# Two decode attentions side by side: part of one weight load and the two output stores move from SP's DMA queue to GpSimd's

## The chip, the cores and the metric

The kernel runs on one core of a Trainium2 chip. The time is device microseconds of one execution; the time of a version is the median of several runs. The runs before took 249.95, 250.19 and 251.74 us, median 250.19. One more execution was taken by the hardware profiler; it took 250.0 us, and its trace gives all other times here.

## What is computed

Two independent attention blocks, A and B, each for one new token (batch 1, one query position) and a model width of 576: project to 32 query heads of 128, attend over 16 heads of a key and value cache (two query heads share one), and project back to 576. A sees the last 2048 positions of its cache, B all 8192. All tensors are bfloat16. The two results are put side by side.

```python
def _A_ref(x, k_cache, v_cache, wq, wo):
    W = min(4096, max(256, Sk // 4))                       # 2048
    q = (x @ wq).reshape(B, Sq, Hq, Dh) ...
    k = jnp.repeat(k_cache[:, :, Sk - W:, :], rep, axis=1)  # B: the whole cache
    v = jnp.repeat(v_cache[:, :, Sk - W:, :], rep, axis=1)
    p = _softmax(jnp.einsum("bhqd,bhkd->bhqk", q, k) * (Dh ** -0.5), axis=-1)
    o = jnp.einsum("bhqk,bhkd->bhqd", p, v)
    return o ... .reshape(B, Sq, Hq * Dh) @ wo
...
return jnp.concatenate([a, b], axis=-1)
```

## The kernel before

The kernel is written by hand, engine by engine. `Prog` (lines 32 to 104) holds one list of operations for each engine; `op` adds a compute instruction and `load` a DMA, each with the names it depends on. `emit` (54) writes the lists out in that order: an engine waits with `wait_ge` for the semaphores that its next instruction needs and has not yet seen. A DMA adds 16 to a semaphore of its own. So the order on each engine, and on the queue that issues its DMAs, is the order of the calls in the source.

**Loads.** All large loads go out from SP. `place` (167) hands out space in `ring`, an area of 144 KB in each of the 128 partitions, in turn; a load waits until the users of what lay there before are done. The order is: A's wq (line 198, the first 512 rows as 128 partitions of 32 KB, and line 200, the other 64 rows as 128 partitions of 4 KB), B's wq in the same two parts, then for each pair of heads p = 0 to 7 the K of B (208, 128 partitions of 32 KB), the K of A (211, twice 4 KB), the V of B, the V of A, and then wo of A (219, one load of 36 KB a partition) and wo of B in six loads, the last two of 1152 bytes a partition. The two x rows, 1152 bytes each, go out from ACT (189).

**GpSimd.** It issues no DMA. It makes the constants at the start (229 to 242): a row of ones, the identity `ident`, then `identf` (235), and the memsets of `zb` (236), `za` (237), `mexp`, `onesf` and `pts` (240), last the permutation `perm` (241).

**Projection.** x is replicated over columns by matmuls with a row of ones (272), after VectorE has doubled the tail of x into `xdup` (263), and copied to `xrep` (275, 278). Then come eight groups of matmuls for A and eight for B (`qmm`, line 295), five matmuls of 512 columns each; they wait for their weights by name (297). ACT and VectorE bring the sums out (301, 304), VectorE transposes them (306) and places them in `za` and `zb` (318, 312). The projections' end frees the ring space of wq, for which SP's load of A's first V (211) waits.

**Attention.** For each pair p VectorE transposes ten slabs of K in the ring (335), PE multiplies them with the queries (345); a maximum, an exponential (380), transposes of the weights (384), the product with V (393, 400) and a fold into `ob` (414, 421) follow.

**End.** After the sums are divided out, PE projects with wo (457), first A, then B in six steps as its loads land. For each of the two, ACT and VectorE copy one row each into `outsb` (465, 468), and SP stores the two rows of 576 bytes (469, `out0` and `out1`). SP's last step (473) waits for both stores.

The steps of the prediction touch the issue of A's wq (198), GpSimd's list (229 to 241), the wait of `qmm` (297) and the stores (469).

Of the kernel before, what the change touches and what calls it, by code (L numbers as in the profile page):

```python
# [31 lines left out]
class Prog:  # L32
# [9 lines left out]
    def op(self, eng, fn, deps=(), name=None):  # L42
        self.ops[eng].append((fn, tuple(deps), name, None))
        if name is not None:
            assert name not in self.where, name
            self.where[name] = (eng, len(self.ops[eng]) - 1)

    def load(self, eng, fn, sem, value, deps=(), name=None):
        self.ops[eng].append((fn, tuple(deps), None, sem))
        if name is not None:  # L50
            assert name not in self.dma, name
            self.dma[name] = (sem, value)
# [54 lines left out]
def bass_concat_heads__sliding_block_cached__gqa_block_cached__decode_kernel(nc, A_x, A_k_cache, A_v_cache, A_wq, A_wo,  # L107
# [51 lines left out]
    op, load = pg.op, pg.load  # L159
    s_x = [nc.alloc_semaphore("s_x%d" % i) for i in range(2)]  # L160
    s_ld = [nc.alloc_semaphore("s_ld%d" % i) for i in range(NSEM)]
    s_out = nc.alloc_semaphore("s_out")


# [2 lines left out]
    def place(size, uses, issue, name):  # L167
        if at[0] + size > RING:
            at[0] = 0
        lo, hi = at[0], at[0] + size  # L170
        at[0] = hi
        deps = []
        for r in list(live):
            if r[0] < hi and lo < r[1]:
                deps += r[2]
                live.remove(r)
        n = nload[0]
        nload[0] += 1
        if n >= NSEM:
            deps += uses_of[n - NSEM]  # L180
        uses_of.append(list(uses))
        live.append((lo, hi, list(uses)))
        t = ring[:, lo:hi]
        load("sp", lambda e: issue(e, t), s_ld[n % NSEM], 16 * (n // NSEM + 1), deps=deps, name=name)
        return t
# [7 lines left out]
    wq_at = {}  # L193
    w = HQ * DH
    for P in range(2):
        uses = ["qmm%d.7" % P]
        main = wqs[P][0:512, :].rearrange("(p k) n -> p (k n)", k=4)
        wq_at[P, 0] = place(4 * w, uses, lambda e, t, main=main: e.dma_start(t, main), "wq%d.0" % P)
        tail = wqs[P][512:DM, :].rearrange("r (c n) -> (r c) n", c=2)
        wq_at[P, 1] = place(w // 2, uses, lambda e, t, tail=tail: e.dma_start(t, tail), "wq%d.1" % P)  # L200

    kv_at = {}
    for p in range(NP):
        for kind, c in (("K", ks), ("V", vs)):
# [3 lines left out]
                                      lambda e, t, src=src: e.dma_start(t, src), "%sB%d" % (kind, p))  # L208
            src = c[0][0, 2 * p:2 * p + 2, SK - W_A:SK, :].rearrange("h (q t) d -> q h (t d)", q=128)
            kv_at[kind, p, 1] = place(2 * SLAB, [use % (p, NI - 1)],  # L210
                                      lambda e, t, src=src: e.dma_start(t.rearrange("q (h n) -> q h n", h=2), src),
# [11 lines left out]
    def slab(kind, p, s):  # L223
# [9 lines left out]
       deps=["id0"], name="ident")  # L233
# [12 lines left out]
    for c in range(2):  # L246
        op("dve", lambda e, c=c: e.tensor_reduce(par[:, c:c + 1], view(identf, 128, c, [[2, 64]]), AX.X, ALU.add),
           deps=["identf"], name="par%d" % c)
    for h in range(2):
        op("dve", lambda e, h=h: e.tensor_reduce(  # L250
            cls[:, 2 * h:2 * h + 2], view(identf, 128, 64 * h, [[1, 2], [32, 2], [2, NB]]), AX.XY, ALU.add),
            deps=["identf"], name="clsB%d" % h)
    op("dve", lambda e: e.tensor_reduce(cls[:, 4:8], view(identf, 128, 2 * NB, [[1, 4], [32, 4]]), AX.X, ALU.add),
       deps=["identf"], name="clsA")
    op("dve", lambda e: e.tensor_reduce(selb[:], view(identf, 128, 0, [[1, 16], [32, 4]]), AX.X, ALU.add),
       deps=["identf"], name="selb")
    op("dve", lambda e: e.tensor_reduce(sela[:], view(identf, 128, 0, [[4, 2], [1, 2], [32, 4], [2, 2]]), AX.XY, ALU.add),
       deps=["identf"], name="sela")
# [3 lines left out]
    for P in range(2):  # L262
# [14 lines left out]
        for c in range(2):  # L277
            op("dve", lambda e, P=P, c=c: e.tensor_scalar(  # L278
                xrep[:, P, 4 + c, :], banks[2 * P + 1][:, 0:128], par[:, c:c + 1], None, ALU.mult),
                deps=["xT%d.4" % P, "par%d" % c], name="xr%d.%d" % (P, 1 + c))  # L280
    XR = ["xr%d.%d" % (P, c) for P in range(2) for c in range(3)]

    KT = NKT * SLAB
    for P in range(2):
        for n in range(8):
            u = 8 * P + n
            bank = banks[u % 4]

            def mm(e, P=P, n=n, bank=bank):
                for k in range(5):  # L290
                    if k < 4:
                        lhsT, o = xrep[:, P, k, :], wq_at[P, 0][:, k * w + n * 512:k * w + (n + 1) * 512]
                    else:
                        lhsT, o = xrep[:, P, 4 + n // 4, :], wq_at[P, 1][:, (n % 4) * 512:(n % 4 + 1) * 512]
                    ins = e.matmul(bank[:, :], lhsT=lhsT, rhs=o, start=(k == 0), stop=(k == 4))  # L295
                return ins
            op("pe", mm, deps=["wq%d.0" % P, "wq%d.1" % P] + XR + (["qe%d" % (u - 4)] if u >= 4 else []),
               name="qmm%d.%d" % (P, n))
            deps = ["qmm%d.%d" % (P, n)] + (["qT%d" % (u - 2)] if u >= 2 else [])
            if n % 2 == 0:  # L300
                op("act", lambda e, n=n, bank=bank: e.activation(qsb[:, n % 2, :], bank[:, :], ACT.Copy),  # L301
                   deps=deps, name="qe%d" % u)
            else:
                op("dve", lambda e, n=n, bank=bank: e.tensor_copy(qsb[:, n % 2, :], bank[:, :]),
                   deps=deps, name="qe%d" % u)
            op("dve", lambda e, n=n: e.transpose(  # L306
                ktb[:, n * 512:(n + 1) * 512].bitcast(I32), qsb[:, n % 2, :].bitcast(I32)),
                deps=["qe%d" % u] + (["z0.%d" % i for i in range(8)] if P else []), name="qT%d" % u)
        srcs = [[512, NP], [64, 2], [1, 2], [128, 2]]
        for b in range(4):  # L310
            if P == 1:
                op("dve", lambda e, b=b: e.tensor_copy(
                    view(zb, NP * 4 * ZW, 32 * b + W0, [[4 * ZW, NP], [2 * ZW, 2], [ZW, 2], [1, 2]], 32, 32 * b),
                    view(ktb, KT, b // 2 * 256, srcs, 32, 32 * b)),
                    deps=["qT%d" % u for u in range(8, 16)] + ["zb0"], name="z1.%d" % b)
            else:
                for h in range(2):
                    op("dve", lambda e, b=b, h=h: e.tensor_copy(
                        view(za, NP * 1024, h * 512 + 32 * b + 2 * (NB + h),
                             [[1024, NP], [256, 2], [128, 2], [1, 2]], 32, 32 * b),  # L320
                        view(ktb, KT, h * 256, srcs, 32, 32 * b)),
                        deps=["qT%d" % u for u in range(8)] + ["za0"], name="z0.%d" % (2 * b + h))
# [6 lines left out]
    for p in range(NP):  # L329
        for s in range(NI):  # L330
            k = p * NI + s
            kt = ktb[:, (k % NKT) * SLAB:(k % NKT + 1) * SLAB]
            deps = [unit("K", p, s)]
            deps += ["S%d" % (k - NKT)] if k >= NKT else Z
            op("dve", lambda e, p=p, s=s, kt=kt: e.transpose(kt.bitcast(I32), slab("K", p, s).bitcast(I32)),  # L335
               deps=deps, name="T%d.%d" % (p, s))
# [12 lines left out]
            deps = ["T%d.%d" % (p, s)]  # L349
# [5 lines left out]
           deps=["S%d" % (p * NI + NI - 1)] + (["mT%d" % (p - 1)] if p else []), name="max%d" % p)  # L355
        op("pe", lambda e: e.matmul(mb[0:1, 0:128], lhsT=mx[:, 0:1], rhs=identf[:, :], start=True, stop=True),  # L356
           deps=["max%d" % p, "identf"] + (["mrA%d" % (p - 1), "mrB1.%d" % (p - 1), "nb%d" % (p - 1)] if p else []),
           name="mT%d" % p)
        deps = ["mT%d" % p] + (["bc%d" % (p - 1)] if p else ["mexp0"])
        for h in range(2):  # L360
            op("dve", lambda e, h=h: e.tensor_reduce(
                mr[0:1, 2 * h:2 * h + 2], view(mb, 512, 64 * h, [[1, 2], [32, 2], [2, NB]], parts=1), AX.XY, ALU.max),
                deps=deps + (["mxB%d.%d" % (h, p - 1)] if p else []), name="mrB%d.%d" % (h, p))
        op("dve", lambda e: e.tensor_reduce(
            mr[0:1, 4:8], view(mb, 512, 2 * NB, [[1, 4], [32, 4]], parts=1), AX.X, ALU.max),
            deps=deps + (["mxA%d" % (p - 1)] if p else []), name="mrA%d" % p)
        for h in range(2):
# [3 lines left out]
                deps=["mrB%d.%d" % (h, p)], name="mxB%d.%d" % (h, p))  # L371
# [3 lines left out]
            deps=["mrA%d" % p], name="mxA%d" % p)  # L375
        op("pe", lambda e: e.matmul(mb[:, 128:129], lhsT=mexp[0:1, :], rhs=onesf[0:1, 0:1], start=True, stop=True),
           deps=["mxA%d" % p, "mxB0.%d" % p, "mxB1.%d" % p, "ones"], name="bc%d" % p)
        op("dve", lambda e, p=p: e.tensor_copy(nb[:, p % 2:p % 2 + 1], mb[:, 128:129]),  # L378
           deps=["bc%d" % p] + (["exp%d" % (p - 2)] if p >= 2 else []), name="nb%d" % p)
        op("act", lambda e, p=p: e.activation(psb[:, :], sb[p % 2][:, :], ACT.Exp, bias=nb[:, p % 2:p % 2 + 1],  # L380
                                              scale=SCALE, accum_out=rsall[:, p:p + 1]),
           deps=["nb%d" % p, "warm1"] + (["PT0.%d" % (p - 1), "PT1.%d" % (p - 1)] if p else []), name="exp%d" % p)
# [67 lines left out]
    for P in range(2):  # L450
        k0 = 0
        for c, kk in enumerate(NWO[P]):
            def mm(e, P=P, c=c, k0=k0, kk=kk):
                for k in range(kk):
                    for n in range(2):
                        r = 32 * (2 * P + n)
                        ins = e.matmul(fb[r:r + 1, 0:288], lhsT=oP[:, 1 - P, k0 + k:k0 + k + 1],  # L457
                                       rhs=wo_at[P, c][:, k * DM + 288 * n:k * DM + 288 * n + 288],
                                       start=(k0 + k == 0), stop=(k0 + k == HQ - 1))
                return ins  # L460
            op("pe", mm, deps=["wo%d.%d" % (P, c), "oP"] + ["qe%d" % u for u in range(16)], name="F%d.%d" % (P, c))
            k0 += kk
        done = "F%d.%d" % (P, len(NWO[P]) - 1)
        r = 64 * P
        op("act", lambda e, r=r: e.activation(outsb[r:r + 1, :], fb[r:r + 1, 0:288], ACT.Copy),
           deps=[done], name="f%d.0" % P)
        r = 64 * P + 32
        op("dve", lambda e, r=r: e.tensor_copy(outsb[r:r + 1, :], fb[r:r + 1, 0:288]), deps=[done], name="f%d.1" % P)
        load("sp", lambda e, P=P: e.dma_start(
            out[0, 0:1, P * DM:(P + 1) * DM].rearrange("o (n c) -> (o n) c", n=2),  # L470
            bass.AP(tensor=outsb, offset=64 * P * 288, ap=[[32 * 288, 2], [1, 288]])),
            s_out, 16 * (P + 1), deps=["f%d.0" % P, "f%d.1" % P], name="out%d" % P)
# [32 lines left out]
```

## Time and profile before

| what | value |
|---|---|
| median of three runs | 250.19 us |
| the profiled execution | 250.0 us |
| its span, from the first to the last instruction | 248.2 us |
| busy: PE, VectorE, ACT, GpSimd | 181.7, 153.1, 18.1, 13.4 us |
| mean DMA rate | 415 GB/s, 102.92 MB |
| mean granted TensorE clock | 0.82 |
| median from issue to landing, K and V of B | 27.0 and 26.8 us |

How to read the profile: times are microseconds from the start of the span. A page has rows of 40 digits, one for each fortieth of the span (6.2 us); a digit is the busy share in tenths, 9 being 90% or more. A row of the timeline has the start, the time, the engine (`PE` matmul, `PEld` weight load, `DVE` VectorE, `POOL` GpSimd, `SPq` the instruction of SP that issues a DMA), the line, the operation with output and input, and in brackets how long the engine had been idle and what released it. The chain of waits is followed back from the last instruction, at each step to what released it. A row of stretches has its bounds and length, the busy time and the number of instructions of PE, weight loads, VectorE, ACT and GpSimd, then the granted clock, the share of the DMA engines, and GB/s.

The chain by lines, as the page sums it up:

```profile
DMA ring<-in_B_k_cache_dram 22%; DVE ktb L335 18%; DMA ring<-in_B_wo_dram 10%; PE sb L345 10%; PE vb L393 7%; DVE xdup L263 5%; PE sb L295 4%; PE qb L295 3%; DVE pts L384 3%; ACT psb L380 2%; PE ob L414 1%; DVE mx L354 1%; PE ob L421 1%; PE vb L400 1%; PE mb L356 1%
```

### The profile page before, as it was taken

The numbers are of one execution on the slowest core, as the hardware profiler recorded it, in microseconds if no ns is written. First come the engines' busy times: TensorE is split into PE (matmuls) and PEld (weight loads), VectorE is DVE, ScalarE is ACT, GpSimd is POOL, SyncE is SP. The second block draws the span as 40 slices with busy tenths as digits, with TensorE's granted clock in tenths as the row PEclk, the third lists the DMA queues.
The fourth block names the chain that finished last, engine by engine and source line by source line (L and its number), as shares of the span: only waits on it lengthen the run. The fifth ranks groups of instructions, "written<-read, shape, count | busy, mean of one in ns | idle before, by whom it ended". The sixth has DMA issues, their size and how long they took to land.

```text
span 248.2 us, 2581 instructions
## 1 busy us (share of the span) xinstructions
PE 181.7 (73%) x1085; PEld 80.7 (33%) x1085; DVE 153.1 (62%) x228; ACT 18.1 (7%) x36; POOL 13.4 (5%) x15
## 2 busy tenths in 40 slices
PE   0039994957995799379746984998489757975795
PEld 0013441313631342143224321732153124322552
DVE  8963779952885298439734873487349725972300
ACT  2001220010001000100010001000100010001000
POOL 8920000000000000000000000000000000000000
PEclk9999999795589599877987597569677957895769
DMA  7999999999999999999999999999999999999992
GB/s 264 418 490 433 422 422 416 417 428 418 427 414 434 419 458 419 436 432 431 421 429 414 434 422 428 420 422 419 433 420 433 428 433 422 436 403 457 395 406 111
DMA packets 8262, 102.92 MB, mean 415 GB/s; under 512 B 694, under 2 KB 956, under 8 KB 5564
## 3 DMA queue, kind: packets, MB, share of 16 engines
q1 hardware_dynamic: 8248, 102.77, 97.9%
q8 instruction: 8, 0.13, 0.2%
q14 instruction: 2, 0.02, 0.0%
q10 hardware_dynamic: 4, 0.00, 0.0%
HBM read 102.76 MB, written 0.00 MB: 414 GB/s over the span
## 4 chain that ended last, share of the span: by engine, by line
DMA 32%; DVE 31%; PE 30%; issue 3%; ACT 2%; SPq 0%; POOL 0%; POOLq 0%; DVEq 0%
DMA ring<-in_B_k_cache_dram 22%; DVE ktb L335 18%; DMA ring<-in_B_wo_dram 10%; PE sb L345 10%; PE vb L393 7%; DVE xdup L263 5%; PE sb L295 4%; PE qb L295 3%; DVE pts L384 3%; ACT psb L380 2%; PE ob L414 1%; DVE mx L354 1%; PE ob L421 1%; PE vb L400 1%; PE mb L356 1%
## 5 line engine op out<-in xcount | busy, mean ns | idle before, releaser
L335 DVE STREAM_TRANSPOSE ktb<-ring 128x1024 int32<-128x1024 int32 x80 | 92.4, 1213 | 11.3 <-DMA ring<-in_B_k_cache_dram 7.6
L345 PE MATMUL sb<-ktb,zb 128*128 128x512 bf16 x256 | 73.6, 443 | 11.0 <-DVE ktb L335 9.8
L345 PEld LDWEIGHTS sb<-ktb,zb 128*128 128x128 bf16 x256 | 25.6, 110 | 56.3 <-DVE ktb L335 24.2
L393 PE MATMUL vb<-ring,pts 128*16 128x512 bf16 x256 | 28.2, 619 | 21.1 <-DVE pts L384 21.1
L409 DVE COPY xo<-vb 128x512 f32<-128x512 f32 x8 | 5.5, 692 | 35.8 <-PE vb L400 35.8
L393 PEld LDWEIGHTS vb<-ring,pts 128*16 128x16 bf16 x256 | 8.5, 123 | 34.3 <-issue 34.2
L345 PE MATMUL sb<-ktb,za 128*128 128x512 bf16 x64 | 16.7, 381 | 1.3
L380 ACT ACTIVATE psb<-sb,nb 128x512 bf16<-128x512 f32 x8 | 5.5, 687 | 140.9 <-DVE nb L378 140.9
L384 DVE STREAM_TRANSPOSE pts<-psb 64x512 bf16<-64x512 bf16 x16 | 11.3, 706 | 7.0 <-ACT psb L380 6.8
L295 PE MATMUL sb<-ring,xrep 128*128 128x512 bf16 x40 | 11.2, 438 | 1.3 <-DVE xrep L278 1.3
L263 DVE COPY xdup<-xrow 1x128 bf16<-1x128 bf16 x2 | 11.3, 5660 | 0.0
L457 PE MATMUL qb<-ring,oP 128*1 128x288 bf16 x128 | 10.9, 346 | 0.5 <-DVE oP L446 0.4
L414 PEld LDWEIGHTS ob<-selb,xo 128*128 128x128 f32 x64 | 10.1, 242 | 3.4 <-ACT xo L407 3.4
L354 DVE TENSOR_REDUCE mx<-sb 128x1 f32<-128x512 f32 x8 | 5.5, 692 | 9.1 <-PE sb L345 9.1
L414 PE MATMUL ob<-selb,xo 128*128 128x4 f32 x64 | 10.8, 293 | 0.3 <-ACT xo L407 0.3
L272 PE MATMUL sb<-onesb,xrow 1*128 1x128 bf16 x4 | 0.6, 295 | 14.0 <-DVE xdup L263 14.0
L306 DVE STREAM_TRANSPOSE ktb<-qsb 128x256 int32<-128x256 int32 x16 | 7.0, 443 | 6.1 <-ACT qsb L301 5.8
L421 PE MATMUL ob<-sela,xo 128*128 128x2 f32 x64 | 9.9, 276 | 0.0
L421 PEld LDWEIGHTS ob<-sela,xo 128*128 128x128 f32 x64 | 9.5, 227 | 0.0
L295 PE MATMUL qb<-ring,xrep 128*128 128x512 bf16 x40 | 9.3, 379 | 0.0
L345 PEld LDWEIGHTS sb<-ktb,za 128*128 128x128 bf16 x64 | 4.9, 96 | 13.1 <-DVE ktb L335 9.2
L457 PEld LDWEIGHTS qb<-ring,oP 128*1 128x1 bf16 x128 | 6.1, 99 | 5.3 <-DMA ring<-in_B_wo_dram 1.2
(66 smaller groups left out, 83.0 us busy)
## 6 DMA issues: line engine op xcount, KB each, us to landing
ring<-in_B_k_cache_dram SPq DMA_DIRECT2D x8, 4096.0 KB, 27.0
ring<-in_B_v_cache_dram SPq DMA_DIRECT2D x8, 4096.0 KB, 26.8
ring<-in_A_k_cache_dram SPq DMA_DIRECT2D x8, 1024.0 KB, 28.9
ring<-in_A_v_cache_dram SPq DMA_DIRECT2D x8, 1024.0 KB, 27.2
ring<-in_A_wo_dram SPq DMA_DIRECT2D x1, 4608.0 KB, 28.2
ring<-in_A_wq_dram SPq DMA_DIRECT2D x1, 4096.0 KB, 12.2
ring<-in_B_wq_dram SPq DMA_DIRECT2D x1, 4096.0 KB, 22.3
ring<-in_B_wo_dram SPq DMA_DIRECT2D x1, 2304.0 KB, 33.4
```

What stands on the lines that cost most here:

```text
L263: op("dve", lambda e, P=P: e.tensor_copy(view(xdup, 256, 128 * P, [[2, 64], [1, 2]], parts=1), view(xrow, 2 * DM, P * DM + 512, [[1, 64], ...
L295: ins = e.matmul(bank[:, :], lhsT=lhsT, rhs=o, start=(k == 0), stop=(k == 4))
L306: op("dve", lambda e, n=n: e.transpose(ktb[:, n * 512:(n + 1) * 512].bitcast(I32), qsb[:, n % 2, :].bitcast(I32)), deps=["qe%d" % u] + ([" ...
L335: op("dve", lambda e, p=p, s=s, kt=kt: e.transpose(kt.bitcast(I32), slab("K", p, s).bitcast(I32)), deps=deps, name="T%d.%d" % (p, s))
L345: ins = e.matmul(sb[p % 2][:, :], lhsT=lhsT, rhs=view(ktb, KT, (k % NKT) * SLAB + 64 * c + v, [[128, 16], [2, 32]]), start=(s == 0 and c = ...
L354: op("dve", lambda e, p=p: e.tensor_reduce(mx[:, 0:1], sb[p % 2][:, :], AX.X, ALU.max), deps=["S%d" % (p * NI + NI - 1)] + (["mT%d" % (p - ...
L380: op("act", lambda e, p=p: e.activation(psb[:, :], sb[p % 2][:, :], ACT.Exp, bias=nb[:, p % 2:p % 2 + 1], scale=SCALE, accum_out=rsall[:, ...
L384: op("dve", lambda e, h=h: e.transpose(view(pts, 1024, 2 * h, [[4, 16], [64, 16], [1, 2]], 64, 64 * h), psb[64 * h:64 * h + 64, :]), deps= ...
L393: ins = e.matmul(vb[0][32 * j:32 * j + 16, :], lhsT=view(pts, 1024, 64 * s + 16 * j, [[1, 16]]), rhs=src[:, 512 * j:512 * j + 512], start= ...
L414: ins = e.matmul(ob[:, 8 * p:8 * p + 4], lhsT=xo[:, 0, 128 * t:128 * t + 128], rhs=selb[:, 4 * t:4 * t + 4], start=(t == 0), stop=(t == 3))
L421: ins = e.matmul(ob[:, 8 * p + 4 + 2 * h:8 * p + 6 + 2 * h], lhsT=xo[:, 1, 256 * h + 128 * t:256 * h + 128 * t + 128], rhs=sela[:, 2 * t:2 ...
L457: ins = e.matmul(fb[r:r + 1, 0:288], lhsT=oP[:, 1 - P, k0 + k:k0 + k + 1], rhs=wo_at[P, c][:, k * DM + 288 * n:k * DM + 288 * n + 288], st ...
```

## The change

The 128 partitions of A's first wq load are divided. SP loads partitions 32 to 127 (3 MB), GpSimd partitions 0 to 31 (1 MB) with a semaphore of its own. GpSimd's load is the first entry of its list, ahead of the constants. All 16 projection groups name it among what they wait for. Both stores are issued by GpSimd, after its constants; SP's last step still waits for them. No other instruction is added, removed or put in another place, and the bytes moved are the same.

```diff
+    s_wq = nc.alloc_semaphore("s_wq")
...
-        wq_at[P, 0] = place(4 * w, uses, lambda e, t, main=main: e.dma_start(t, main), "wq%d.0" % P)
+        p0 = 32 if P == 0 else 0
+        wq_at[P, 0] = place(4 * w, uses, lambda e, t, main=main, p0=p0: e.dma_start(t[p0:, :], main[p0:, :]),
+                            "wq%d.0" % P)
+        if p0:
+            load("pool", lambda e, t=wq_at[P, 0], main=main, p0=p0: e.dma_start(t[0:p0, :], main[0:p0, :]),
+                 s_wq, 16, name="wq0.p")
...
-            op("pe", mm, deps=["wq%d.0" % P, "wq%d.1" % P] + XR + (["qe%d" % (u - 4)] if u >= 4 else []),
+            op("pe", mm, deps=["wq%d.0" % P, "wq%d.1" % P, "wq0.p"] + XR + (["qe%d" % (u - 4)] if u >= 4 else []),
...
-        load("sp", lambda e, P=P: e.dma_start(
+        load("pool", lambda e, P=P: e.dma_start(
```

## The prediction

> **What bounds the kernel now.** I read the page first, then the chain of waits, then the end of the run in one-microsecond stretches, then the first stretch of the timeline on GpSimd, VectorE and SP. The page, with its slices of the span and its DMA queues:
>
> ```profile
> span 248.2 us, 2581 instructions
> PE   0039994957995799379746984998489757975795
> DMA  7999999999999999999999999999999999999992
> q1 hardware_dynamic: 8248, 102.77, 97.9%
> ```
>
> The reader is to see that the 16 DMA engines are full from the second slice to the last but one, that nearly all of it is one queue (SP's, 102.77 MB), and that PE has gaps in every part. That is 6.42 MB for each engine. The trace's packet records give the pace: a 32 KB packet takes 1.21 us, which is 27 GB/s for an engine and 432 GB/s for the 16. At that pace 102.77 MB are 238 us of the 248.2; the rest is the start (first packet at 1.78 us, all first packets over at 4.09), the 4 KB packets (0.160 us where the 32 KB pace would give 0.152; 272 of them for an engine, 2.3 us), and the end.
>
> The chain of waits, its last pieces (start, us, what), and the end of the run in stretches (the next to last figure of a row is the share of the DMA engines):
>
> ```profile
> 219.43 25.99 DMA ring<-in_B_wo_dram
> 245.42 0.04 issue
> 245.47 0.30 PE qb L457 x2
> 245.79 0.46 DVE outsb L468
> ```
>
> ```profile
> 242.00:243.00 1.00, 1.00 (x22) 0.72 (x18) 0.13 (x1) 0.08 (x1) 0.00 (x0) 1.00 0.95 365
> 243.00:244.00 1.00, 1.00 (x18) 0.57 (x14) 0.00 (x0) 0.00 (x0) 0.00 (x0) 1.00 0.57 214
> 244.00:245.00 1.00, 0.96 (x14) 0.35 (x12) 0.00 (x0) 0.00 (x0) 0.00 (x0) 1.00 0.32 112
> ```
>
> The end hangs on the last load: it lands at 245.42, two matmuls, a copy of 0.46, and the output follow. The engines do not finish together: the share falls from 0.95 to 0.57 to 0.32, and the 16 completion marks of the last load are seven between 243.09 and 243.45 and nine between 244.67 and 245.42. So the latest engine sets the time, seven engines have some 2 us to spare, and nine have little or none.
>
> **The change, part by part.** The timeline (start, us, engine, line, operation) gives the rows to cost it by:
>
> ```profile
> 0.74 0.39 SPq L198 DMA_DIRECT2D ring<-in_A_wq_dram  x1
> 0.34 0.10 POOL L490 MEMSET const-uint8-127<- 128x1 uint8 x1
> 2.78 11.12 DVE L263 COPY xdup<-xrow 1x128 bf16<-1x128 bf16 x1
> 12.87 0.95 POOL L240 MEMSET pts<- 128x1024 bf16 x1
> 15.78 0.20 DVE L263 COPY xdup<-xrow 1x128 bf16<-1x128 bf16 x1
> 18.10 4.28 PE L295 MATMUL sb<-ring,xrep 128*128 128x512 bf16 x10 [1.28 <-DVE xrep L278]
> 28.89 0.38 SPq L211 DMA_DIRECT2D ring<-in_A_v_cache_dram  x1
> 208.57 4.62 DVE L335 STREAM_TRANSPOSE ktb<-ring 128x1024 int32<-128x1024 int32 x4 [1.81 <-DMA ring<-in_B_k_cache_dram]
> 246.33 0.49 SPq L469 DMA_DIRECT2D out_dram<-outsb  x1
> ```
>
> *The bytes.* 1 MB leaves SP's first DMA and goes out by GpSimd's; SP keeps 96 partitions. The total stays 102.77 MB, so at the pace of the engines the stream stays as long: 0, if each engine still gets 256 KB of the two parts. The rows allow that: 96 and 32 partitions over 16 engines are six and two packets of 32 KB each, where the 128 are eight now. SP's first issue stays at 0.74 and its first packet at 1.78. GpSimd's issue cannot pass the same start barrier (its first instruction is at 0.73), so it starts nothing sooner; the most it can gain is that a late engine is fed earlier. The first packets start between 1.78 and 2.87, so that is a gain of at most 1.1 us, and 0 by the fact that all of them end within 0.5 us (3.57 to 4.09) whenever they began. I take 0.
>
> [...]
>
> *The issue on GpSimd.* The new DMA stands ahead of onesb, ident and the memsets, and GpSimd has no DMA in this trace. Lower bound: SP's issue, 0.39 us. Upper bound, an estimate: one shortest GpSimd step (0.10) for each of 32 rows, 3.2 us. I take 1.6, one step for each of the 16 engines. All GpSimd work moves later by that. Who waits: VectorE's first reductions (2 us into the run), ACT's first exponential, and the first xdup copy, which takes 11.12 us where its twin takes 0.20 and ends at 13.90, just after the memset of pts (12.87 + 0.95 = 13.82). So it waits out GpSimd's run of memsets and moves by the same 1.6, and with it the x replication on PE and the projection from 18.10 to 19.7. What hides it: the projection frees ring space for SP's issue at 28.89, which would be at 30.5, and the loads already queued last until B's first V lands (48.68). The cover is 18 us. Compute itself has caught up long before the end: at 208.57 the transposes wait for the load, not the other way (1.81 us). Cost 0; without the cover 1.6.
>
> *The added wait.* The projections wait for GpSimd's part as well. Behind that wait stands all of PE's queue, and behind PE the evictions on ACT and VectorE and SP's slot at 28.89. It ends late only if GpSimd's packets land after 18.1. The nearest row is x of B by ACT's queue: issued at 1.28, its packet ran at 6.17, between SP's packets. Two packets for each engine among SP's give some 6 to 13 us: cost 0.
>
> *The outputs.* out0 (issue at 242.21) lies beside B's matmuls and costs nothing on either queue. out1 is on the end: the copy is over at 246.26, SP issues at 246.33, the last completion mark is at 247.83. Of these 1.50 us, 0.37 are the packet itself (starts at 247.46) and 1.13 the issue side. On GpSimd that side cannot go below one step of 0.10, a gain of 1.0; above, 16 steps of 0.10 in place of the 0.49 of SP's instruction give 1.6 - 0.5 = 1.1 more. [...] SP's final wait and the closing barrier stay.
>
> [...]
>
> Sum: 0 + 0 + 0 + 0.5. The profiled execution took 250.0 us (span 248.2 and 1.8 around it), 0.2 below the median of 250.19, so 250.5 for it and **250.7 us** as a median. From the bounds (-1.0 and -0.3 at the start; +1.1) this case spans 249.4 to 251.5.
>
> **Rivals.** *Uneven engines (slower).* The split of the first load into 96 and 32 partitions need not fall on the engines as the 128 did. If an engine of the late group gets two packets more, or two engines hold each other up in writing the same partitions, it falls back by 2 x 1.21 = 2.4 us; by twice that with four packets. Nothing brings it back: the engines are full to the end, and the last load is split evenly. The place is A's wq, between 2 and 13 us; it decides once a late engine loses anything, or an early one more than 2 us. For: the 0.95, 0.57, 0.32 of the end show that a lag of one engine is still there at the end. Against: 96 and 32 both divide by 16. Time: 250.7 + 2.4 = 253.1, to 255.5. [...]
>
> *A small gain.* The engines that start last (2.87) get GpSimd's packets sooner, and out1 is no slower by GpSimd: up to 0.5 + 0.5 off, 249.2 to 249.9. Against: the first packets end together.
>
> *The parts do not overlap.* If GpSimd's packets were served only after all that SP has queued, the projection would start near 48.7 and not 18.1, SP's slot at 28.89 would come near 59.5, and the engines would be empty for some 11 us: 262. The interleaved packet at 6.17 speaks against it.
>
> **Numbers.** Forecast case 0.48; small gain 0.13; uneven engines 0.36; starved part 0.03. The likeliest case's own range is 249.4 to 251.5; with most of the uneven engines' case the range is 249.4 to 254.8. A measurement of this kernel tells about 1% (2.5 us) from no change: above 252.7 lie the starved part and nine tenths of the uneven case, 0.35; below 247.7 only a gain that no row prices, 0.03; within, 0.62.
>
> **What would show it.** Right: the DMA row stays at nines, the completion marks of the last load end at 245.4 ± 0.4 in the same two groups, the time from the last copy to out1's mark is about 2.1 us, the first xdup copy ends 1 to 3 us later with no idle time in the DMA row at 40 to 60 us. Wrong by engines: marks of A's wq spread over more than the 0.5 us of now (12.44 to 12.95), packets longer than 1.21 us in the first 13 us, and a last load that lands after 247. Wrong by the output: more than 3 us, or under 1, from copy to mark. Wrong by the added wait: a projection that starts after 22 us with the DMA named as its releaser.

## The result, and the profile after

The changed kernel takes 260.74 us in the median of four runs (259.37 to 261.75), beside 250.07 before: a ratio of 1.041 [1.033, 1.048] (in brackets the 95% interval, here and below). Six more runs later gave 259.68 us (259.38 to 260.20) and 1.038 [1.036, 1.041]. It is slower by 3.8 to 4.1%, 9.6 us in the later runs and 10.7 in the first four, where 0.5 us was forecast and 254.8 us was the end of the range.

Lines of the page of the changed kernel, with its slices of the span (6.5 us each) and its queues (q0 is GpSimd's):

```profile
span 260.0 us, 2583 instructions
DMA  9999999999999999999999999999999999999980
GB/s 217 232 197 383 386 471 419 412 412 470 406 416 440 435 403 424 454 396 433 413 459 391 464 415 422 433 447 396 437 436 424 413 420 453 401 446 428 404 323 5
q1 hardware_dynamic: 8208, 101.71, 95.1%
q0 software_dynamic: 112, 1.05, 1.8%
```

The same row of the kernel before:

```profile
GB/s 264 418 490 433 422 422 416 417 428 418 427 414 434 419 458 419 436 432 431 421 429 414 434 422 428 420 422 419 433 420 433 428 433 422 436 403 457 395 406 111
```

The reader is to see that the DMA row does not show the loss: its digits are nearly all nines in both. The row of GB/s shows it: in the first three slices (0 to 19.5 us) the engines, busy for 90% or more of each slice, move 217, 232 and 197 GB/s where they moved 264, 418 and 490. From the fourth slice on the two are close. The trace's packet records (one record for each piece that an engine moves, with its queue, size and times) say more: a 32 KB packet of A's wq takes 2.0 to 2.5 us for the most part, on both queues, and 32 KB packets take 1.22 from 22 us on, where 1.21 was the time before. Some 16 packets are in flight at any moment in both kernels, as many as there are engines. The first part of A's wq, as SP loads it, is complete at 22.65 us and not at 12.95, and each of the large loads behind it is late by 9.1 to 9.7 us.

The rows of the timeline that answer to those of the prediction:

```profile
1.27 0.64 POOL L203 DMA_DIRECT2D ring<-in_A_wq_dram  x1 [0.83 <-POOLq L496]
3.95 11.12 DVE L269 COPY xdup<-xrow 1x128 bf16<-1x128 bf16 x1
23.78 3.95 PE L301 MATMUL sb<-ring,xrep 128*128 128x512 bf16 x10 [5.79 <-DMA ring<-in_A_wq_dram]
34.23 0.38 SPq L217 DMA_DIRECT2D ring<-in_A_v_cache_dram  x1
217.75 4.62 DVE L341 STREAM_TRANSPOSE ktb<-ring 128x1024 int32<-128x1024 int32 x4 [2.09 <-DMA ring<-in_B_k_cache_dram]
258.00 0.54 POOL L475 DMA_DIRECT2D out_dram<-outsb  x1 [2.88 <-DVE outsb L474]
```

The eighth K of B is ready at 217.75 and not at 208.57: 9.2 us, nearly what was lost at the start. So hardly anything was lost on the way and hardly anything was made up. The end of this profile is longer by another 2.6 us. The stores are one part (below). The other belongs to this execution, one of the two longer ones of its four: its chain ends in PE's 128 matmuls of the output projection and not in a load. In the profile of the six later runs the eighth K is ready at the same time (217.68), but that projection starts at 243.49 and not at 246.59. The clock granted to TensorE between the two points was lower in the first; why it was is not shown. Stretches of the first (bounds and length; PE, weight loads, VectorE, ACT, GpSimd; granted clock, DMA share, GB/s):

```profile
217.70:231.40 13.70, 12.18 (x40) 4.21 (x40) 11.74 (x10) 0.00 (x0) 0.00 (x0) 0.75 1.02 431
231.40:246.50 15.10, 9.48 (x72) 6.05 (x71) 5.04 (x16) 1.38 (x3) 0.00 (x0) 0.63 0.99 425
246.50:257.00 10.50, 10.34 (x128) 6.28 (x128) 0.47 (x2) 0.43 (x2) 0.54 (x1) 0.72 0.56 221
```

and of the later one:

```profile
217.70:231.40 13.70, 11.30 (x42) 3.76 (x42) 12.16 (x11) 0.00 (x0) 0.00 (x0) 0.88 1.03 433
231.40:246.50 15.10, 9.90 (x96) 5.85 (x97) 4.35 (x15) 1.38 (x3) 0.00 (x0) 0.75 0.98 420
246.50:257.00 10.50, 8.02 (x106) 4.24 (x100) 0.91 (x2) 0.80 (x2) 1.08 (x2) 0.88 0.60 240
```

The clock is 0.75, 0.63, 0.72 in the one and 0.88, 0.75, 0.88 in the other, and the busy time of PE in the first stretch is 12.18 us for 40 matmuls and 11.30 for 42. The chain of waits of the later profile ends like that of before, in a load:

```profile
228.26 26.30 DMA ring<-in_B_wo_dram
254.56 0.04 issue
254.61 0.31 PE qb L463 x2
254.91 0.02 issue
254.94 0.47 DVE outsb L474
255.41 0.02 issue
255.44 0.02 POOLq L78
255.45 0.48 issue
255.93 0.56 POOLq L481
```

Last load 254.56 against 245.42: 9.1 us. From the last copy to the store's completion mark 2.13 us against 1.57: 0.56. Together 9.7, which is the difference of the spans (257.9 and 248.2).

### The profile page after: what moved, and what is told of

It reads as the page before. It is cut to its first block, busy times and chain, and to the rows that moved or that the text cites. A ratio compares the mean times of both kernels' runs of the same rounds, so it can differ in the third digit from the quotient of the medians.

```text
span 260.0 us, 2583 instructions
## 1 busy us (share of the span) xinstructions
PE 183.7 (71%) x1085; PEld 82.2 (32%) x1085; DVE 153.6 (59%) x228; ACT 18.1 (7%) x36; POOL 15.1 (6%) x18
## 4 chain that ended last, share of the span: by engine, by line
DMA 41%; PE 33%; DVE 20%; issue 3%; ACT 2%; POOLq 0%; SPq 0%; DVEq 0%
DMA ring<-in_B_k_cache_dram 32%; DVE ktb L341 13%; PE sb L351 10%; DMA ring<-in_A_wq_dram 9%; PE vb L399 7%; PE sb L301 4%; PE qb L463 4%; PE qb L301 3%; DVE pts L390 3%; ACT psb L386 2%; PE ob L420 1%; DVE mx L360 1%; PE ob L427 1%; PE mb L362 1%; PE mb L382 1%
## 5 line engine op out<-in xcount | busy, mean ns | idle before, releaser
L351 PE MATMUL sb<-ktb,zb 128*128 128x512 bf16 x256 | 75.1, 455 | 14.4 <-DVE ktb L341 13.7
L351 PEld LDWEIGHTS sb<-ktb,zb 128*128 128x128 bf16 x256 | 26.5, 111 | 60.3 <-DVE ktb L341 25.4
L475 POOL DMA_DIRECT2D out_dram<-outsb x2 | 1.1, 538 | 242.1 <-DVE outsb L474 242.1
L312 DVE STREAM_TRANSPOSE ktb<-qsb 128x256 int32<-128x256 int32 x16 | 7.1, 445 | 11.1 <-ACT qsb L307 10.7
L463 PE MATMUL qb<-ring,oP 128*1 128x288 bf16 x128 | 10.3, 346 | 0.4 <-DVE oP L452 0.4
```

Source lines behind the costliest of these rows:

```text
L312: op("dve", lambda e, n=n: e.transpose(ktb[:, n * 512:(n + 1) * 512].bitcast(I32), qsb[:, n % 2, :].bitcast(I32)), deps=["qe%d" % u] + ([" ...
L351: ins = e.matmul(sb[p % 2][:, :], lhsT=lhsT, rhs=view(ktb, KT, (k % NKT) * SLAB + 64 * c + v, [[128, 16], [2, 32]]), start=(s == 0 and c = ...
```

## The experiments

Two theories were left by the profile. **S (shape):** a load that does not cover all partitions is slow by itself. **Q (queues):** two queues on the same engines disturb each other. The first slow packets ran before GpSimd's first one (7.84 us), which speaks for S, but GpSimd had issued its load by then (1.27 us). Four kernels, each the kernel before with one edit (where A's wq is divided, the projection groups wait for all parts, as in the change):

**Both parts from SP**

```diff
+        p0 = 32 if P == 0 else 0
+        wq_at[P, 0] = place(..., lambda e, t, main=main, p0=p0: e.dma_start(t[p0:, :], main[p0:, :]), ...)
+            load("sp", lambda e, ...: e.dma_start(t[0:p0, :], main[0:p0, :]), s_wq, 16, name="wq0.p")
```

> A's first wq load is divided into partitions 32 to 127 and 0 to 31 as in the changed kernel, but both parts go out from SP, one after the other, and the stores stay on SP. GpSimd has no DMA. Theory S (shape): a load that covers 96 or 32 partitions runs its packets at about half pace, whoever issues it. Then 32 KB packets take 2.0 to 2.5 us, A's wq lands at 20 to 23 us and not at 12.9, and the time is 258 to 261 us. Theory Q (two queues): it is the second queue on the same DMA engines that halves the pace. Then packets stay at 1.21 us and the time is 249.5 to 250.7 us.

Measured 259.37 us, 1.035 [1.031, 1.039]. Its row of GB/s:

```profile
GB/s 209 209 229 325 412 437 397 451 397 463 438 411 411 451 433 411 416 448 430 412 422 416 451 397 442 410 457 388 453 422 435 407 447 414 437 440 419 412 401 111
```

The loss is there with no DMA on GpSimd: 209, 209, 229, with packets of 2.1 to 2.6 us up to 20 us. S holds for these blocks, and Q is not needed for the loss.

**The same 1 MB from GpSimd, as columns**

```diff
+        p0 = w if P == 0 else 0
+        ... e.dma_start(t[:, p0:], main[:, p0:])                            # SP: 24 KB of each partition
+            load("pool", lambda e, ...: e.dma_start(t[:, 0:p0], main[:, 0:p0]), s_wq, 16, name="wq0.p")
```

> The same 1 MB goes out from GpSimd's queue, but as the first 8 KB of all 128 partitions; SP loads the other 24 KB of all 128. The stores stay on SP. Theory S: packets of both queues keep the pace of 27 GB/s (24 KB in 0.91 us, 8 KB in 0.30 us, where they do not share an engine), A's wq lands by 13.5 us, time 249.5 to 250.8 us. Theory Q: half pace as long as both queues have packets, time 256 to 261 us.

Measured 250.09 us, 1.000 [0.998, 1.002]. Its row:

```profile
GB/s 263 417 465 438 443 422 421 410 429 416 428 417 424 421 444 417 456 416 433 418 437 417 424 422 438 419 422 418 433 419 443 427 422 422 435 414 445 404 401 107
```

Two queues run side by side at full rate: 24 KB packets take 0.91 us and 8 KB packets 0.31, and some 16 packets are in flight at any moment, as with one queue. The second queue costs nothing here and brings nothing: Q falls.

**The stores alone**

```diff
-        load("sp", lambda e, P=P: e.dma_start(
+        load("pool", lambda e, P=P: e.dma_start(
```

> Only the two stores move to GpSimd's queue; wq is loaded as before. Both theories: nothing before the last copy changes, and the end is longer by what the two profiles show between the last copy's end and the end of the span (2.5 us against 2.0): plus 0.5 to 0.6 us, 250.4 to 250.9 us. If GpSimd's 1 MB had a hand in the slow store, it is plus 0.0 to 0.3.

Measured 250.47 us beside 250.06, 1.001 [0.999, 1.003]: 0.4 us in the medians, which the interval does not part from nothing. Its profile shows the step more closely (last copy, then the issue; the copy ends at 246.15):

```profile
245.69 0.46 DVE L468 CAST outsb<-qb 1x288 bf16<-1x288 f32 x1 [3.96 <-PE qb L457]
246.72 0.54 POOL L469 DMA_DIRECT2D out_dram<-outsb  x1 [3.71 <-DVE outsb L468]
```

SP issued 0.08 us after the copy, GpSimd 0.57 us after it; from copy to completion mark it is 2.15 us against 1.57.

**The wq part alone** (the change without the edit of the stores)

> Only the wq part of the change: 96 partitions from SP, 32 from GpSimd; the stores stay on SP. Both theories: the whole change less the 0.5 to 0.6 us of the stores, 258.5 to 260.5 us. If it comes out under 256, the stores and the load act together and both theories lack something.

Measured 259.04 us, 1.034 [1.030, 1.038]. With the stores' 0.4 that is 259.4, and the whole change, run again, confirms the sum:

**The whole change again**

> The changed kernel once more, with more rounds, because its four runs lay in two groups (259.4 and 259.8; 261.6 and 261.8 us). If load and stores add up, 250.05 + 9.0 (wq part alone) + 0.4 (stores alone) gives 259.4 to 259.8 as the usual run, with some runs 2 us above, as the kernel before has too (251.7 to 252.2 beside 250.0). If the two parts act on each other, most runs lie at 261 and above.

Measured 259.68 us, none of six runs over 260.2. The parts add up.

**Which shapes are slow.** The next question is why. Extra loads ahead of the kernel's own, each alone on the engines:

```diff
+    for i, (p0, p1, step, n) in enumerate([...]):
+        load("sp", lambda e, ...: e.dma_start(hole[p0:p1:step, 0:n], wide[p0:p1:step, 0:n]), s_pr[i], 16, deps=last, ...)
+        last = ("pr%d" % i,)
```

> Ahead of the loads, SP issues eleven extra loads of wq rows (32 KB each; the first, a warm-up, 8 KB) into ring space that is not yet in use, each after the one before has landed, so each has the DMA engines to itself: all 128 partitions; partitions 32 to 127; 0 to 63; 0 to 31; 0 to 15; 0 to 7; 0, 4 ... 28; 0 to 111; every second of the 128; every fourth. The kernel's time grows by their sum and tells nothing. Theory P (places): packets are slow because several DMA engines write at the same time into partitions that share a way in. [...] Theory R (count): whatever is not all 128 partitions runs at half pace for another reason (rows for each engine, the reading side); then 0 to 7 and 0, 4 ... 28 take the same time, and 0 to 15 no longer than 0 to 31.

The stretches from a load's first packet to its last completion mark, in the order of the text above, without the warm-up; the last figure is GB/s:

```profile
6.44:17.89 11.45, 1.38 (x10) 0.91 (x10) 9.91 (x8) 0.00 (x0) 7.71 (x5) 1.00 0.90 366
18.88:34.31 15.43, 0.00 (x0) 0.00 (x0) 0.00 (x0) 0.00 (x0) 0.00 (x0) 1.00 0.89 204
35.68:47.19 11.51, 0.00 (x0) 0.00 (x0) 0.00 (x0) 0.00 (x0) 0.00 (x0) 1.00 0.87 182
48.17:54.50 6.33, 0.00 (x0) 0.00 (x0) 0.00 (x0) 0.00 (x0) 0.00 (x0) 1.00 0.74 160
55.48:60.79 5.31, 0.00 (x0) 0.00 (x0) 0.00 (x0) 0.00 (x0) 0.00 (x0) 1.00 0.69 99
61.70:67.25 5.55, 0.00 (x0) 0.00 (x0) 0.00 (x0) 0.00 (x0) 0.00 (x0) 1.00 0.30 41
68.77:71.16 2.39, 0.00 (x0) 0.00 (x0) 0.00 (x0) 0.00 (x0) 0.00 (x0) 1.00 0.37 110
72.12:87.58 15.46, 0.00 (x0) 0.00 (x0) 0.00 (x0) 0.00 (x0) 0.00 (x0) 1.00 0.92 237
88.92:95.21 6.29, 0.00 (x0) 0.00 (x0) 0.00 (x0) 0.00 (x0) 0.00 (x0) 1.00 0.85 328
96.50:100.41 3.91, 0.00 (x0) 0.00 (x0) 0.00 (x0) 0.00 (x0) 0.00 (x0) 1.00 0.77 268
```

The packet records of the same loads, median time of a 32 KB packet:

| partitions | packets | us a packet |
|---|---|---|
| all 128 | 128 | 1.21 |
| 32 to 127 | 96 | 2.30 |
| 0 to 63 | 64 | 2.56 |
| 0 to 31 | 32 | 2.54 |
| 0 to 15 | 16 | 3.69 |
| 0 to 7 | 8 | 3.95 |
| 0, 4 ... 28 | 8 | 1.78 |
| 0 to 111 | 112 | 2.12 |
| 0, 2 ... 126 | 64 | 1.21 |
| 0, 4 ... 124 | 32 | 1.21 |

The loads of 16 and 8 partitions consist of first packets alone, and a load's first packets take 1.8 to 1.9 us in these probes even at full pace (eight by fours: 1.78; the first 16 packets of the kernel before: 1.21 to 2.18, median 1.94).

Theory R falls: eight partitions by fours take 2.39 us from start to mark and eight neighbours 5.55, with as many packets and completion marks; 64 and 32 partitions by twos and fours run at full pace (1.21 us a packet) where 64 and 32 neighbours run at about half (2.56 and 2.54). What counts here is which partitions a load takes at the same time, and not how many. Theory P fits the rows, if neighbours are what shares a way in; no run shows the way in by itself. For 0 to 15 and 0 to 7 the records say 3.7 to 4.0 us a packet; from first packet to last mark these two take 5.3 and 5.6 us, 3 us above the eight by fours. In these two loads the last mark comes 1.3 and 1.4 us after the last record's end, against 0.3 to 0.4 with all 128 partitions and with the eight by fours, so the records alone understate them.

One rival was not varied alone. Each probe, and each split of A's wq, reads the rows of wq that belong to the partitions it writes, so a block of neighbours is also read from one piece of DRAM. The trace of the kernel before speaks against the reading side: the last 64 rows of A's wq are 512 KB in one piece, as much as the probe of 0 to 15 reads, but they go to all 128 partitions, and their 4 KB packets take 0.16 us, which is 26 GB/s for an engine beside the 27 of full pace. No run read scattered rows into neighbouring partitions, so that it is the writing and not the reading is likely but not shown.

**The probes from GpSimd**

> The same probes from GpSimd's queue: all 128 partitions, 32 to 127, 0 to 63, 0 to 31, 0 to 15, 32 KB rows, each alone. The constants stand behind them on GpSimd and the time tells nothing. Theory P: the queue does not matter, 1.2, 2.4, 2.4, 2.4 and 4.8 us a packet. If GpSimd's DMA were slow by itself, the 128 partitions would also be over 1.5.

Measured 1.21, 2.35, 2.56, 2.55 and 3.66 us a packet: within 0.05 us of SP's. The queue does not matter here. The 4.8 us expected for 0 to 15 was the author's estimate; no run shows it.

**Halves: neighbours, and by twos**

```diff
+        SP:      e.dma_start(t[64:, :], main[64:, :])          GpSimd: e.dma_start(t[0:64, :], main[0:64, :])
...
+        SP:      e.dma_start(t[1::2, :], main[1::2, :])        GpSimd: e.dma_start(t[0::2, :], main[0::2, :])
```

> A's first wq load as two halves, partitions 64 to 127 from SP and 0 to 63 from GpSimd, the stores on SP. Theory P: in step, all 16 engines write into one half at a time, 2.4 us a packet and 258 to 260 us; if the two queues get the engines out of step, so that half of them write into each half of the partitions, packets take 1.2 to 1.8 and the time is 250 to 254 us. Theory R: 258 to 260 us.

> The two halves once more, 64 partitions from SP and 64 from GpSimd, the stores on SP, but the odd partitions from SP and the even ones from GpSimd, where the halves before were 64 to 127 and 0 to 63. Theory P: 1.2 to 1.3 us a packet, 249.7 to 250.7 us. Theory R: 258 to 261 us, as the contiguous halves.

Measured 260.42 us, 1.043 [1.039, 1.047], for the neighbours (packets 2.4 to 2.56 us on either queue after the first), and 250.22 us, 1.000 [0.998, 1.003], by twos (1.21 us a packet after the first). The rows of GB/s, neighbours and then by twos:

```profile
GB/s 163 243 177 309 406 472 376 444 404 468 382 454 413 462 406 420 432 445 413 421 446 416 418 414 458 381 453 408 455 387 447 432 435 404 446 409 442 419 406 136
GB/s 254 433 422 467 435 427 426 416 429 417 427 412 429 417 427 424 442 420 454 419 431 411 436 420 435 419 428 424 427 420 422 422 438 427 430 406 463 392 406 120
```

Queues, bytes and counts are the same; only the step of the partitions, and of the rows read for them, differs, and it is worth 10.2 us. The records also show that the two queues do not mix in the halves: the packets start in rounds of 16, all of one queue. With neighbours 16 of GpSimd's start between 9.19 and 10.28 us and then 16 of SP's between 11.59 and 12.65, so all packets in flight lie in one half of the partitions.

**Quarters: the change's own counts, by fours**

```diff
+            wq_at[P, 0] = place(..., lambda e, t, main=main: e.dma_start(t[1::4, :], main[1::4, :]), "wq0.0")
+            for j in (2, 3):
+                load("sp", lambda e, ...: e.dma_start(t[j::4, :], main[j::4, :]), s_wq[j], 16, ...)
+            load("pool", lambda e, ...: e.dma_start(t[0::4, :], main[0::4, :]), s_wq[0], 16, name="wq0.p")
```

> A's first wq load again as 32 partitions from GpSimd and 96 from SP, the stores on SP, but interleaved: GpSimd takes partitions 0, 4 ... 124, SP three loads of 32 that start at 1, 2 and 3, also by fours. Theory P (places), after the probe in which 32 partitions by fours ran at 1.21 us a packet: 1.2 to 1.3 us a packet, A's wq lands by 13.5 us, 249.7 to 250.7 us. Theory R (count of partitions) and any effect of the second queue: 256 us and more.

Measured 250.30 us, 1.001 [0.998, 1.004], packets 1.21 to 1.25 us after the first. With the stores on GpSimd as well:

> The whole change with the interleaved quarters in place of the blocks: GpSimd loads 32 partitions by fours, SP the other three quarters, GpSimd issues both stores. Theory P: the crowding is gone, the stores' 0.4 us stays: 250.4 to 250.9 us, not faster than before.

Measured 250.67 us, 1.002 [1.000, 1.004]. The whole change made with spread partitions costs 0.6 us in the medians, with an interval that just reaches no change; that is near what was forecast for the change as it stands. No version was faster than the kernel before.

## Why the prediction was wrong

*The bytes: the step that failed.* "The total stays 102.77 MB, so at the pace of the engines the stream stays as long: 0, if each engine still gets 256 KB of the two parts." The condition seems to have been met: the packets start in six rounds of 16 of SP's and two of GpSimd's, though the records do not name the engine. What failed is the pace: 1.21 us was read off 128-partition loads and taken for a property of the engine. It holds for loads spread over the 128 partitions, and not for a block of 96 or 32 neighbours (2.30 and 2.54 us in the probes). At 2.3 us for each of eight packets the term, put at 0, is 8 x (2.3 - 1.21) = 8.7 us, and A's wq was late by 8.2 (first mark) to 9.7 us (last). The split on SP, the columns, the probes and the halves show it; that the engines meet at the writing side of the partitions is inferred.

*The rival.* "Two engines hold each other up in writing the same partitions" comes near what is inferred here, and "Nothing brings it back" is what happened: 9.2 us at the eighth K, 9.1 at the last load. It was priced as an accident of one or two engines, two to four packets, 2.4 to 4.8 us; in fact the packets of both parts are slow through the whole load. The argument against it, that 96 and 32 divide by 16, is about counts, and counts turned out not to matter. The even split of the trace before had no row for it.

*The gain at the start.* 0, as taken. GpSimd's issue ran at 1.27 us, not with the barrier at 0.73, and its first packet at 7.84.

*GpSimd's issue.* 1.6 us taken; the work moved by 1.17 (the first xdup copy starts at 3.95 and not 2.78, and takes the same 11.12). Hidden, as argued: SP's slot came at 34.23 with loads queued until 57.9.

*The added wait.* The projection began at 23.78, released by wq. That is the sign named for "wrong by the added wait", but the part that came last was SP's own (marks to 23.69; GpSimd's to 20.49). The wait cost nothing of its own; the columns kernel has it and takes 250.09.

*The outputs.* +0.5 stands in the sum without a row of before under it: the rows gave only bounds, -1.0 and +1.1. No run shows that figure; the runs showed 0.56 to 0.58 in the profiles and 0.4 in the medians in its place, so the size was met. GpSimd's instruction takes 0.54 us beside SP's 0.49, and the time is lost before it, 0.5 us more between the copy's end and the instruction's start.

*The range.* The bounds of the likeliest case were added to the wrong base: -1.0 and +1.1 price the stores against the kernel before, so with the -0.3, which no row gives, they span 248.9 to 251.3 and not 249.4 to 251.5. The result lies outside either.

*The other rivals.* Neither came: no version gained, and GpSimd's packets ran between SP's (from 7.84 us), not behind all of them.

*The signs.* The DMA row stayed at nines, as the prediction said it would if right, in a kernel that lost 9 us there. The marks of A's wq spread over 2.0 us (20.65 to 22.65) against 0.5, packets were longer than 1.21 us, and the last load landed after 247: the three signs of uneven engines, all met. They did not tell uneven engines from packets that are all slow alike: marks 2.0 us apart in a load that is 8.2 to 9.7 us late say that most of the loss was common to the engines.

## What to carry to other kernels

Here a DMA's pace depended on which partitions it took at one time. A load of a contiguous block of 112, 96, 64 or 32 partitions ran at about half pace (2.1 to 2.6 us for 32 KB, against 1.21), and 64 or 32 partitions taken by twos or fours over all 128 ran at full pace; 16 or 8 neighbours took 3.7 to 4.0 us for a first packet, against 1.78. So to divide such a load, divide its columns (250.09 us here) or interleave its partitions (250.22 by twos, 250.30 by fours). In this kernel, which keeps the DMA engines full, time lost in one load was not made up (9.1 us of it was left at the last load), and a busy row that stays at nines did not show it: read GB/s beside it.

## What the runs showed of the hardware

Two queues with packets waiting lost nothing by it here: 250.09 us with 1 MB on GpSimd's, beside 250.06 before, at 0.31 and 0.91 us for 8 and 24 KB, and some 16 packets in flight as with one queue.

The last store, issued by GpSimd, landed 2.13 and 2.15 us after the copy's end, against 1.57 when SP issued it: later by 0.56 to 0.58 us, nearly all of it between the end of the wait and the start of the instruction (0.48 us in the chain of waits above, at 255.45).

How a load's rows are given to the engines can't be read from these traces, which do not name the engine. Why 32 to 127 take 2.30 us a packet, 0 to 111 2.12 and 0 to 15 3.7 is not shown by any run.
